# A planned residual quantizer: one PSUM pool, larger score tiles, strict turns on the DMA queues

## The chip, the cores and the metric

The kernel runs on one core of a Trainium2 chip. The metric is the device time of one execution in microseconds. The core has five engines that run side by side: TensorE (PE in the profile, its weight loads PEld), VectorE (DVE), ScalarE (ACT), GpSimd (POOL) and SyncE (SP). Each carries out its own instructions in the order in which they were written, and waits for the others by semaphores. Sixteen DMA engines, which all queues share, move data between the device memory and the on-chip memory (SBUF). Matmul results go to PSUM, a small memory of eight banks of 2 KB a partition, from which DVE or ACT must take them away.

## The reference

Two signals of 16,000 tokens with 512 features pass through a three-tap convolution over time, feature by feature, and SiLU. Four stages of vector quantization follow: each finds the nearest of eight code words to what is left, and subtracts it. The sum of the chosen words goes through a second three-tap convolution.

```
xp = jnp.pad(x, ((0,0),(pad,pad),(0,0)))
for i in range(K):                       # K = 3
    z = z + xp[:, i:i+T, :] * dw_enc[i][None, None, :]
z = jax.nn.silu(z)
res = z; q = 0
for s in range(Nq):                      # Nq = 4 stages, C = 8 words each
    cb = codebooks[s]
    d2 = |res|^2 - 2 res.cb + |cb|^2     # [B, T, C]
    sel = cb[d2.argmin(-1)]
    q = q + sel; res = res - sel
qp = jnp.pad(q, ((0,0),(pad,pad),(0,0)))
for i in range(K):
    y = y + qp[:, i:i+T, :] * dw_dec[i][None, None, :]
```

(x is 2 x 16,000 x 512; everything is bf16.)

## The kernel before, in words

The 32,000 tokens are laid out as 128 partitions of 250 consecutive tokens. A *group* g is the g-th token of every partition, so 128 tokens; a *chunk* is up to 16 groups (`SIZES`: 12, then fourteen times 16, then 14). The 512 features are four tiles of 128.

*Loading.* `XT` holds a chunk and one more group on either side with features on the partitions. It comes by transposing DMAs on SP's queue (L486), four groups to a DMA, so five a chunk with the last one half as large; `xpool` has two `XT`. The first chunk comes another way: `XR` is loaded as it lies (L291, one DMA on SP's queue, and the two edge pieces on ACT's, L294), PE transposes it (L454) into PSUM, and ACT (L461) and DVE (L459) copy it to `XT`, two of the four feature tiles each.

*Front, a chunk and feature tile at a time.* Three products with the taps on DVE (L553), two sums, either on DVE (L561) or as an accumulating DMA from POOL's queue (L559; all four first sums and one of the second sums in every chunk but the first, so 75 in all), Exp, Ln and Exp on ACT (L565, L573, L576) with an addition of one on DVE between (L569), and the product on DVE (L581), which gives the residual `RES`.

*A stage.* `score` (L629) multiplies, on PE, each half group of residuals with itself and with the code words beside it; a large negative mask (L637) leaves only the diagonal in play, so that a maximum (L651, DVE) is the squared length. L654 copies the dot products. Short DVE instructions (L673 to L697) make the one-hot of the nearest word; PE transposes it (L707), DVE copies it to `OHT` (L714). Then the word is subtracted for each pair of quarter chunks and feature tile: either PE adds both in PSUM (L752, L731, tile `NEW`) and ACT copies the result back (L758), or PE makes only the word (`SEL`) and DVE adds (L747). `ON_DVE` says how many go each way.

*Output.* `finish` multiplies the one-hots with tables of decoder tap times code word (L785, tile `Y`), ACT copies to `YSB` (L791), SP stores four groups at once (L795).

*PSUM.* `psG` has two tiles of one bank for scores, with up to `GB` = 6 groups each, so a 16-group stage uses three (6, 5, 5). `psA` has three tiles of two banks for all else.

*The order* is written out by a planner. Each piece of work is a task with an engine, a guessed cost, what it needs, which buffers it takes and gives back, and a due time. `Plan.run` schedules all tasks forward and backward several times with random shifts (`ROUNDS`: seed, spreads, passes), and `emit` writes the instructions in the order of the planned starts. On the queues shared by transposes and accumulating DMAs the planner asks for a distance `APART` between the two kinds. `keep_apart` (L409) makes it a real dependency: a DMA of one kind waits for the one `LAG` places back among those of the other kind already written. Where the plan leaves PE idle, `emit` fills in matmuls whose results nobody reads (L430), if a score bank is planned free and PE was planned busy for less than `WARM` of the last 4 us; `ahead` does the same once at the start (L439).

Of the kernel before, what the change touches and what calls it, by code (L numbers as in the profile page):

```python
# [21 lines left out]
GB = 6  # L22
# [10 lines left out]
WARM = 0.6  # L33
# [8 lines left out]

ZB, TB, EB, LNB, YB = 4, 5, 3, 1, 3
# [3 lines left out]
ROUNDS = [(940, 0.3, 0.0, 7), (4101, 0.3, 2.0, 9), (5991, 0.3, 0.0, 7), (15520, 0.3, 0.0, 10)]  # L47
# [6 lines left out]
APART, CLUMP = 0.5, 2.0  # L54

LAG = 2


class Plan:
# [18 lines left out]
    def pass_over(self, rank, backward=False):  # L78
# [99 lines left out]
    def emit(self, starts, order):  # L178
        tasks = self.tasks
        free, back, spans, end = self.slots["psG"], [], [], 0.0  # L180
        for n in order:
            engine, hold, delay, _, _, emit, take, give, _, _ = tasks[n]
            at = starts[n]
            if engine == "PE":
                while end + 0.3 <= at:
# [3 lines left out]
                    while spans and spans[0][1] < end - 4.0:  # L189
                        spans.pop(0)  # L190
                    if free > 0 and sum(b - max(a, end - 4.0) for a, b in spans) < 4.0 * WARM and self.idle():
                        spans.append((end, end + 0.3))
                        end += 0.3
                    else:
                        end += 0.1
# [5 lines left out]
            free -= take.count("psG")  # L201
            for _ in range(give.count("psG")):
                heapq.heappush(back, at + max(hold, delay))
# [4 lines left out]
def kernel(  # L208
# [32 lines left out]
    psG = ctx.enter_context(tc.tile_pool(name="psG", bufs=2, space=bass.MemoryType.PSUM))  # L241
    psA = ctx.enter_context(tc.tile_pool(name="psA", bufs=3, space=bass.MemoryType.PSUM))
# [25 lines left out]
    def tap_columns():  # L268
        pst = psA.tile([P, 2, 512], F32, name="ps_w", tag="psa")
# [6 lines left out]
    plan = Plan({"XT": 2, "Z": ZB, "T": TB, "E": EB, "LN": LNB, "Y": YB, "psG": 2, "psA": 3, "RES": 3, "KEY": 3,  # L276
# [22 lines left out]
    def code_words():  # L299
        pst = psA.tile([P, 2, 512], F32, name="ps_cbt", tag="psa")  # L300
# [13 lines left out]
    def code_norms():  # L314
# [12 lines left out]
        psg = psA.tile([P, 2, 512], F32, name="ps_g", tag="psa")  # L327
# [69 lines left out]
    ident, book = landed(1.8), landed(9.3)  # L397
    taps_in = setup(0.2, 0.4, [ident, landed(3.0)], early, tap_columns)
# [24 lines left out]
    pending = []  # L423

    def warm():
        if not scored[2:]:
            return False
        if not pending:
            pending.append(psG.tile([P, 512], F32, name="PS"))
        nc.tensor.matmul(pending[0][:, 0:GB * HT].rearrange("p (r c) -> p r c", c=HT), lhsT=IDENT, rhs=MASK, start=True, stop=True,  # L430
                         skip_group_check=True)
# [4 lines left out]
    def ahead():  # L436
        pending.append(psG.tile([P, 512], F32, name="PS"))
        for _ in range(AHEAD):
            nc.tensor.matmul(pending[0][:, 0:P], lhsT=IDENT, rhs=IDENT, start=True, stop=True, skip_group_check=True)  # L439

    plan.add("PE", 0.1 * AHEAD, 0.1 * AHEAD, [taps_in], early, ahead)

    def load_rows(st, org):
# [6 lines left out]
        def turn(i):  # L450
            pst = psA.tile([P, 2, 512], F32, name="ps_x", tag="psa")
            st["ps", i] = pst.rearrange("p b n -> p (b n)").bitcast(BF16)
            for n in range(G + 2):
# [9 lines left out]
        rows = st["rows"] = plan.add("LOAD", 0.0, 1.2 + 0.46 * (G + 2), [], early, room, take=("XT",))  # L463
        for i in range(KT):
            t = plan.add("PE", 0.11 * (G + 2), 0.11 * (G + 2) + 0.2, [rows, ident], early, lambda i=i: turn(i),
                         take=("psA",))
# [423 lines left out]
```

## Time and profile before

| | us |
|---|---|
| median of the three timed runs | 745.02 (744.42 to 745.52) |
| profiled execution | 742.04 |
| its span | 740.3 |
| DVE busy | 685.9 |
| ACT busy | 665.4 |
| PE busy, weight loads | 590.8, 314.2 |
| POOL busy | 81.7 |
| mean granted PE clock | 0.934 |

The span runs from the first to the last instruction of the execution. Busy is the time in which an engine carries out at least one instruction; of PE it says little, since its matmuls are pipelined. In a group's row the columns are the line, engine and operation, output and input with their shapes, the count, then busy time and mean duration of one in ns, then the idle time of the engine just before them and what ended it. A wait's row gives who waited for whom, the total in us, how often, and the longest.

### The profile page before, as it was taken

Reading aid. Unit: us, or ns where it says so; the run is one execution under the profiler, and the core shown is the slowest. Engines: PE = TensorE matmul, PEld = TensorE weight load, DVE = VectorE, ACT = ScalarE, POOL = GpSimd, SP = SyncE. Lnnn points to the kernel's source line nnn. Section 1 sums busy time; section 2 is a strip of 40 time slices with the busy share of each in tenths; the row PEclk is TensorE's granted clock in tenths of the full one; section 3 lists DMA queues with packets and bytes.
Section 4 is the critical chain, followed back from the end, with each engine's and each line's share of the span. In section 5 each row is a group of like instructions: output and inputs, shape, how many; then the busy total and the mean of one; then the engine's idle time right before and its main releaser. Section 6 shows DMA issues by size and latency. Waiting matters only on the chain. (4 is left out here: it accounts for less than half of the span.)

```text
span 740.3 us, 23586 instructions
## 1 busy us (share of the span) xinstructions
PE 590.8 (80%) x10478; PEld 314.2 (42%) x10544; DVE 685.9 (93%) x1359; ACT 665.4 (90%) x539; POOL 81.7 (11%) x104
## 2 busy tenths in 40 slices
PE   5037687787987888986978888878988898989996
PEld 5023334344444444434444444444453444444543
DVE  6999989899999999997999999989999999998952
ACT  2688979899999999998899999989999999976576
POOL 3112101111101011100101111100111101100000
PEclk9566969999999999999799899999999999999999
DMA  7969795859696967839978875959896435320234
GB/s 178 189 130 182 135 200 104 141 122 201 182 174 158 209 133 164 165 116 143 188 171 177 175 165 143 182 132 174 172 210 136 131 64 152 87 88 2 88 143 199
DMA packets 160833, 111.14 MB, mean 150 GB/s; under 512 B 142426, under 2 KB 142811, under 8 KB 160603
## 3 DMA queue, kind: packets, MB, share of 16 engines
q1 hardware_dynamic: 148976, 69.61, 39.5%
q0 software_dynamic: 11472, 39.76, 29.9%
q8 instruction: 82, 1.34, 0.8%
q10 hardware_dynamic: 282, 0.26, 0.1%
q14 instruction: 21, 0.16, 0.1%
HBM read 2.39 MB, written 32.77 MB: 47 GB/s over the span
## 5 line engine op out<-in xcount | busy, mean ns | idle before, releaser
L758 ACT ACTIVATE RES<-NEW 128x1024 bf16<-128x1024 f32 (+1 forms) x218 | 218.5, 1043 | 28.6 <-PE NEW L731 21.9
L747 DVE TENSOR_TENSOR RES<-RES,SEL 128x1024 bf16<-128x1024 bf16 (+1 forms) x166 | 197.5, 1203 | 6.7 <-PE SEL L731 6.3
L643 PE MATMUL PS<-RES 128*64 128x80 bf16 (+1 forms) x8064 | 176.1, 203 | 11.2 <-DVE RES L581 9.7
L643 PEld LDWEIGHTS <-RES 128*64 128x64 bf16 x8064 | 172.8, 115 | 19.6 <-DVE RES L581 10.6
L752 PE MATMUL NEW<-RES,IDENT 128*128 128x512 bf16 (+1 forms) x436 | 137.7, 399 | 31.3 <-ACT RES L758 15.6
L791 ACT ACTIVATE YSB<-Y 128x1024 bf16<-128x1024 f32 (+1 forms) x126 | 126.6, 1061 | 8.4 <-PE Y L785 4.5
L565 ACT ACTIVATE E<-Z 128x2048 bf16<-128x2048 bf16 (+1 forms) x64 | 123.2, 1931 | 11.5 <-DMA Z<-T 4.0
L559 POOL DMA_DIRECT2D Z<-T x75 | 72.9, 976 | 537.5 <-ACT RES L758 78.8
L573 ACT ACTIVATE LN<-E 128x2048 f32<-128x2048 bf16 (+1 forms) x64 | 123.0, 1923 | 9.9 <-DVE E L569 9.2
L576 ACT ACTIVATE E<-LN 128x2048 bf16<-128x2048 f32 (+1 forms) x64 | 123.0, 1922 | 0.4
L651 DVE TENSOR_REDUCE TR<-PS 128x5 bf16<-128x320 f32 (+1 forms) x188 | 96.0, 515 | 14.4 <-PE PS L643 14.3
L553 DVE TENSOR_SCALAR T<-XT,WENC 128x2048 bf16<-128x2048 bf16 (+1 forms) x128 | 94.8, 745 | 5.1 <-DMA Z<-T 5.1
L731 PEld LDWEIGHTS <-CBN 32*128 32x128 bf16 x768 | 32.6, 92 | 137.7 <-issue 134.3
L785 PE MATMUL Y<-A,OHT 128*128 128x512 bf16 x219 | 77.6, 382 | 16.4 <-ACT RES L758 6.0
L731 PE MATMUL NEW<-OHT,CBN 32*128 32x512 bf16 (+1 forms) x436 | 88.3, 402 | 0.1
L581 DVE TENSOR_TENSOR RES<-Z,E 128x2048 bf16<-128x2048 bf16 (+1 forms) x64 | 77.3, 1208 | 0.0
L731 PE MATMUL SEL<-OHT,CBN 32*128 32x512 bf16 (+1 forms) x332 | 58.7, 396 | 22.0 <-ACT RES L758 13.3
L637 PE MATMUL PS<-MASK,IDENT 128*64 128x320 bf16 (+1 forms) x376 | 64.6, 340 | 8.6 <-DVE PR L654 6.2
L561 DVE TENSOR_TENSOR Z<-Z,T 128x2048 bf16<-128x2048 bf16 (+1 forms) x53 | 62.5, 1181 | 2.7 <-DMA Z<-T 2.7
L752 PEld LDWEIGHTS <-IDENT 128*128 128x128 bf16 x436 | 33.1, 99 | 67.4 <-issue 57.4
L430 PE MATMUL PS<-MASK,IDENT 128*128 128x384 bf16 x167 | 46.2, 359 | 10.1 <-DVE PR L654 9.8
L785 PEld LDWEIGHTS <-OHT 128*128 128x128 bf16 x373 | 32.1, 97 | 50.8 <-issue 22.8
(78 smaller groups left out, 416.2 us busy)
## 6 DMA issues: line engine op xcount, KB each, us to landing
Z<-T POOLq DMA_DIRECT2D x75, 512.0 KB, 5.6
out_dram<-YSB SPq DMA_DIRECT2D x61, 512.0 KB, 3.2
RES<-in_x_dram SPq DMA_DIRECT2D x1, 1664.0 KB, 6.8
XT<-in_x_dram SPq DMA_TRANSPOSE x74, 5.7
out_dram<-YSB SPq DMA_DIRECT2D x1, 384.0 KB, 2.3
out_dram<-YSB SPq DMA_DIRECT2D x1, 256.0 KB, 2.7
A<-in_dw_dec_dram POOLq DMA_DIRECT2D x2, 96.0 KB, 6.4
CB<-in_codebooks_dram ACTq DMA_DIRECT2D x1, 128.0 KB
```

The source lines that it names most:

```text
L553: nc.vector.tensor_scalar(out=places(u[name]), in0=taps(i, k), scalar1=WENC[:, i, k:k + 1], scalar2=None, op0=ALU.mult)
L565: nc.scalar.activation(u["E"][:, 0:G, :], u["Z"][:, 0:G, :], ACT.Exp, scale=-1.0)
L573: nc.scalar.activation(u["LN"][:, 0:G, :], u["E"][:, 0:G, :], ACT.Ln)
L576: nc.scalar.activation(u["E"][:, 0:G, :], u["LN"][:, 0:G, :], ACT.Exp, scale=-1.0)
L643: nc.tensor.matmul(V[h * HT:(h + 1) * HT, r, :], lhsT=half[:, LC:LC + HT], rhs=half[:, lo:hi], start=False, stop=(i == KT - 1), skip_group ...
L651: nc.vector.tensor_reduce(out=u["TR"][:, q:q + m], in_=u["V", q][:, :, own:own + HT], axis=AX.X, op=ALU.max)
L731: nc.tensor.matmul(ps, lhsT=CBN[s][rows, i * P:(i + 1) * P], rhs=u["OHT"][rows, 0:MB, :], start=start, stop=True, skip_group_check=True)
L747: nc.vector.tensor_tensor(out=old, in0=old, in1=u["SEL", i, j][:, :, 0:W].rearrange("p h (m t) -> p h m t", t=HT), op=ALU.add)
L752: nc.tensor.matmul(NEW[:, h, 0:W], lhsT=IDENT, rhs=tokens(i, j + h, 1), start=True, stop=False, skip_group_check=True)
L758: nc.scalar.activation(old, u["NEW", i, j][:, :, 0:W].rearrange("p h (m t) -> p h m t", t=HT), ACT.Copy)
L785: nc.tensor.matmul(Y[:, h, :], lhsT=lhs(), rhs=rhs, start=(a == 0), stop=(a == len(terms) - 1))
L791: nc.scalar.activation(u["YSB"][:, k:k + n, :], u[k][:, 0:n, :], ACT.Copy)
```

## The change

- PSUM is one pool `psA` of four tiles of two banks. `bank(name)` gives every user its tile; it returns the tile that a filler matmul has opened, if there is one.
- `GB` is 4 groups to a bank, and a score tile has two banks: 16 groups take two tiles of 8, 12 take two of 6. The reduction and the copy each run over both banks at once.
- `LAG` is 1: a transpose waits for the last accumulating DMA written before it, and the other way round. The planner's `APART` has a value for each kind, and its costs for a run of transposes are lower.
- The rows of the first chunk come in two halves on SP's queue, after the two edge pieces, which have moved there from ACT's queue. PE transposes the first half of each feature tile when that has come. One of the four copies to `XT` is DVE's, three are ACT's.
- Filler matmuls are 512 columns wide, take a tile of the common pool, and are put in if PE was planned busy for less than 0.75 of the last 3.4 us. `ahead` no longer waits for the taps.
- Seeds, and guessed costs of loads, are new, so the order of work is new on every engine.

```diff
-GB = 6
+GB = 4
-WARM = 0.6
+WARM, WINDOW, TICK = 0.75, 3.4, 0.22
+FIRST_ROWS, ALL_ROWS = 7.8, 10.0
-ROUNDS = [(940, 0.3, 0.0, 7), (4101, 0.3, 2.0, 9), (5991, 0.3, 0.0, 7), (15520, 0.3, 0.0, 10)]
+ROUNDS = [(667, 5.0, 0.0, 4), (2210, 0.3, 2.0, 7), (7052, 1.0, 0.0, 2)]
-APART, CLUMP = 0.5, 2.0
-LAG = 2
+APART = (0.0, 1.9, 2.3)
+CLUMP = 2.0
+LAG = 1
...
-                                lost = max(0.0, APART - (now - ended))
+                                lost = max(0.0, APART[sort if backward else kind] - (now - ended))
...
-    psG = ctx.enter_context(tc.tile_pool(name="psG", bufs=2, space=bass.MemoryType.PSUM))
-    psA = ctx.enter_context(tc.tile_pool(name="psA", bufs=3, space=bass.MemoryType.PSUM))
+    psA = ctx.enter_context(tc.tile_pool(name="psA", bufs=4, space=bass.MemoryType.PSUM))
+    pending = []
+    def bank(name):
+        return pending.pop() if pending else psA.tile([P, 2, 512], F32, name=name, tag="psa")
...
-    nc.sync.dma_start(out=XR[:, 1:G + 2, :], in_=xv[:, 0:G + 1, :])
     for b in range(B):
         p = b * HB
-        nc.scalar.dma_start(out=XR[p + 1:p + HB, 0, :], in_=xv[p:p + HB - 1, S - 1, :])
+        nc.sync.dma_start(out=XR[p + 1:p + HB, 0, :], in_=xv[p:p + HB - 1, S - 1, :])
+    HALF = (G + 2) // 2
+    for a, b in ((1, HALF), (HALF, G + 2)):
+        nc.sync.dma_start(out=XR[:, a:b, :], in_=xv[:, a - 1:b - 1, :])
...
-        nc.tensor.matmul(pending[0][:, 0:GB * HT].rearrange("p (r c) -> p r c", c=HT), lhsT=IDENT, rhs=MASK, start=True, stop=True,
-                         skip_group_check=True)
+        nc.tensor.matmul(pending[0][:, 0, :], lhsT=IDENT, rhs=CB4, start=True, stop=True, skip_group_check=True)
...
-            if i % 2:
+            if i == 0:
                 nc.vector.tensor_copy(st["XT"][:, 0:G + 2, i, :], src)
...
-                done.append(plan.add("DMA", 0.7 * m, 2.7 + 0.7 * m, [room], due, lambda n=n, m=m: run(n, m), mode=RUNS))
+                done.append(plan.add("DMA", 0.6 * m, 2.4 + 0.6 * m, [room], due, lambda n=n, m=m: run(n, m), mode=RUNS))
...
-            PS = pending.pop() if pending else psG.tile([P, 512], F32, name="PS")
-            V = u["V", q] = PS[:, 0:m * (hi - lo)].rearrange("p (r c) -> p r c", r=m)
-            for h in range(2):
-                nc.tensor.matmul(V[h * HT:(h + 1) * HT, :, own:own + HT], lhsT=IDENT[:, h * HT:(h + 1) * HT], rhs=MASK[:, 0:m, :],
-                                 start=True, stop=False, skip_group_check=True)
+            PS = bank("PS")
+            V = u["V", q] = PS[:, :, 0:m // 2 * (hi - lo)].rearrange("p b (r c) -> p b r c", c=hi - lo)
+            for b in range(2):
+                for h in range(2):
+                    nc.tensor.matmul(V[h * HT:(h + 1) * HT, b, :, own:own + HT], lhsT=IDENT[:, h * HT:(h + 1) * HT],
+                                     rhs=MASK[:, 0:m // 2, :], start=True, stop=False, skip_group_check=True)
...
-            nc.vector.tensor_reduce(out=u["TR"][:, q:q + m], in_=u["V", q][:, :, own:own + HT], axis=AX.X, op=ALU.max)
+            nc.vector.tensor_reduce(out=u["TR"][:, q:q + m].rearrange("p (b r) -> p b r", b=2), in_=u["V", q][:, :, :, own:own + HT], axis=AX.X, op=ALU.max)
...
-            nc.vector.tensor_copy(u["PR"][:, q:q + m, :], u["V", q][:, :, pick:pick + C])
-        banks = -(-G // GB)
+            nc.vector.tensor_copy(u["PR"][:, q:q + m, :].rearrange("p (b r) c -> p b r c", b=2), u["V", q][:, :, :, pick:pick + C])
+        banks = -(-G // (2 * GB))
```

All other users of PSUM (`ps_w`, `ps_cbt`, `ps_g`, `ps_x`, `ps_oh`, `SEL`, `NEW`, `Y`) call `bank` in place of `psA.tile`.

More of the change, by code (lines that the diff above doesn't have):

```diff
@@ L188, in emit @@
                         heapq.heappop(back)
-                    while spans and spans[0][1] < end - 4.0:
+                    while spans and spans[0][1] < end - WINDOW:
                         spans.pop(0)
[L191 to L195, printed above, removed]
+                    if (free > 0 and "psA" in take and sum(b - max(a, end - WINDOW) for a, b in spans) < WINDOW * WARM
+                            and self.idle()):
+                        spans.append((end, end + TICK))
+                    end += TICK
                 while back and back[0] <= at:
@@ L200, in emit @@
                 spans.append((at, end))
-            free -= take.count("psG")
-            for _ in range(give.count("psG")):
+            free -= take.count("psA")
+            for _ in range(give.count("psA")):
                 heapq.heappush(back, at + max(hold, delay))
```

64 lines of the change are left out of this document (33 added, 31 removed).

## The prediction

> **What bounds the kernel now.** I read the page's busy table first, then the same by stages, then what the two full engines wait for, then the DMA landings, then the granted clock. The page, with its two rows of slices for clock and DMA:
>
> ```profile
> span 740.3 us, 23586 instructions
> PE 590.8 (80%) x10478; PEld 314.2 (42%) x10544; DVE 685.9 (93%) x1359; ACT 665.4 (90%) x539; POOL 81.7 (11%) x104
> ...
> PEclk9566969999999999999799899999999999999999
> DMA  7969795859696967839978875959896435320234
> ```
>
> VectorE (DVE) is nearly full and ScalarE (ACT) almost as full. The table by stretches says where the rest is:
>
> ```profile
> 0.00:60.00 60.00, 20.94 (x235) 16.48 (x235) 52.37 (x109) 36.07 (x23) 14.85 (x31) 0.71 0.83 166
> 60.00:340.00 280.00, 231.41 (x4197) 119.80 (x4216) 273.10 (x530) 269.49 (x214) 31.99 (x35) 0.94 0.79 157
> 340.00:360.00 20.00, 14.73 (x171) 6.15 (x169) 14.62 (x29) 15.43 (x13) 2.58 (x3) 0.74 1.08 185
> 360.00:623.00 263.00, 222.51 (x4107) 119.28 (x4139) 256.94 (x503) 255.62 (x208) 29.18 (x33) 0.97 0.73 156
> 623.00:740.30 117.30, 101.21 (x1785) 52.50 (x1792) 88.84 (x192) 88.76 (x85) 3.11 (x3) 0.99 0.30 105
> ```
>
> Columns: stretch and length, busy time of PE, weight loads, DVE, ACT, POOL, then clock, DMA share, GB/s. From 60 to 623 us DVE idles 18.3 us and ACT 22.5 us of 563: two engines bound it jointly, and relief of one is worth only what the other follows. The start costs ACT 23.9 us; the tail costs each 28.5 us, a chain through PE. The waits, of DVE, ACT and SP's queue:
>
> ```profile
> DVE T L553 <- DMA Z<-T: 5.1, 4, 4.2
> DVE Z L561 <- DMA Z<-T: 2.7, 2, 2.5
> ```
> ```profile
> ACT RES L758 <- PE NEW L731: 21.9, 24, 2.4
> ACT E L565 <- DMA Z<-T: 4.0, 2, 2.5
> ```
> ```profile
> SPq L486 <- DMA Z<-T: 100.7, 18, 13.7
> ```
>
> Late accumulating DMAs ("adds") cost 11.8 us on the two full engines; SP's 100.7 us before transposes is hidden by the double buffer XT. The landings (SP's transposes, then POOL's adds):
>
> ```profile
> L486 SPq DMA_TRANSPOSE XT<-in_x_dram x74: 1232/3008/8887, 9.4 to 554.9; - x74
> DMA to landing us min/median/max: 3.4/5.7/10.2
> ```
> ```profile
> DMA to landing us min/median/max: 4.5/5.6/12.3
> ```
>
> An add alone lands in 4.5 us, a four-group transpose in 4.5 (3.4 is a two-group one); medians 1.1 to 1.2 above and maxima of 10 to 12 are what they cost each other. The 12.3 us add was issued at 333.5, 0.3 us behind a transpose; with it DVE stood 4.2 us at 345.8, the largest hole of the middle.
>
> **The change part by part.** Working against the profiled execution: 742.04 us, span 740.3 and 1.7 around it. The three timed runs have a median of 745.02, so 3.0 are added at the end.
>
> *Score tiles of 8 groups.* A 16-group stage has two reductions (L651) and two copies (L654) in place of three each (6, 5, 5); the 12-group chunk's 6 and 6 stay.
>
> ```profile
> L651 DVE TENSOR_REDUCE TR<-PS 128x5 bf16<-128x320 f32 x120 | 58.6, 492 | 8.2 <-PE PS L643 8.1
> L651 DVE TENSOR_REDUCE TR<-PS 128x6 bf16<-128x384 f32 x68 | 37.8, 556 | 6.3 <-PE PS L643 6.2
> ...
> L654 DVE CAST PR<-PS 128x40 bf16<-128x40 f32 x120 | 23.7, 198 | 0.0
> ...
> L654 DVE CAST PR<-PS 128x48 bf16<-128x48 f32 x68 | 14.0, 206 | 0.0
> ```
>
> A group more costs a reduction 64 ns and a copy 8, so eight cost 684 and 222 ns. DVE's next instruction starts some 0.09 us before the last one ends (152.74 + 0.49 against 153.14 in the timeline), so by occupied time a stage falls from 0.47 + 2 x 0.40 + 0.12 + 2 x 0.11 = 1.61 us to 2 x (0.59 + 0.135) = 1.45. 60 stages x 0.16 = 10 us less on DVE. ACT gets no relief, so the worth lies between 0 and -10; because ACT has 22.5 us of idle to give up there, I take -6. The coarser last tile is exposed where a stage runs alone: 64 matmuls in place of 40 (0.65 us) is +0.4, reduction and copy +0.2, less the reduction that no longer queues (-0.4): +0.2 us in some five tail stages, +1 (0 to +3). PE: mask columns stay 2,048 a stage, in 8 matmuls for 6; PE is no bound there. Nothing.
>
> *One pool of four double tiles.* Before: three for residuals, one-hots and outputs, two single banks for scores; now a score tile waits in the same queue as the rest. PE's waits for buffers (matmuls behind ACT's or DVE's eviction) sum to about 80 us, mostly harmless; 21.9 us of ACT's own waits for NEW could shrink, or grow when a score tile holds a slot for some 3 us. Occupancy by rows: 8 score tiles x 3 us, 14 NEW x 2.5, 10 SEL x 2.2, 8 Y x 2.5 and 4 one-hots x 1 make 105 of 4 x 42 us a chunk, 62%; before 81 of 3 x 44, 61%. Zero, bounds -6 to +6.
>
> *Strict turns.* Each transpose waits for the last add issued, each add for the last transpose (before: for the one before the last). In the changed order the kind changes 67 times, before 53. Prices: three transposes with nothing beside them took SP 6.49 us (295.17), 2.2 each, half runs 1.25; adds in a row land 2.75 apart (302.39 and 304.07 land at 307.31 and 310.06); a turn adds landing less pace, 1.8 to 2.3. Sum: 59 x 2.2 + 15 x 1.25 + 75 x 2.75 + 67 x 2.0 = 489 us, against some 600 us of DVE work until the last Exp: 31 us a chunk, up to 40 in some, of 40 to 44. It fits, with little left. Queued behind the waits: on SP the stores (4 a chunk) and later transposes, on POOL the next adds; DVE waits for adds (T buffers, Z) and ACT for Z. Best: the 11.8 us of late adds go. Worst: stores, 2.6 us each alone, lie wholly between the turns: 31 + 10 = 41 a chunk, in the six fullest 50, of which the Z and T buffers cover half: +15. I take -4: a third of the late adds goes, since they came from overlap that can't happen now.
>
> By the Trainium skill (DMA: Bandwidth & Descriptors, Rules for kernel authors) a transpose beside ordinary DMAs needs no wait; by that rule this part would buy nothing and cost its turns, and the sum would be some 4 us higher or more. The rows agree on throughput: a transpose and an add issued together at 461.6 and 462.1 both land at 469.8, 8.2 us, against 9.0 in turn. They disagree on spread, as the 12.3 us shows.
>
> *First rows in halves.* Before, PE's transposes waited until 9.26 us for edge rows queued last, and DVE stood 5.63 us until 11.17 behind ps_cbt. Now edges go first and PE starts on half. DVE's order puts code norms (1.75 us), the second code columns (1.2) and one copy of XT (1.0) ahead of the products and loses the other copy (1.0) to ACT, where 1.66 us more fall into its idle start. With code words landed at 8.5 us as before, products begin near 15.1 instead of 13.7, but 4.9 us of work are done: -3.5 (bounds -5 to +1).
>
> *Warm-up matmuls.* The order has 79 of 512 columns for 167 of 384, and 73 of the 79 belong to the first three chunks; the middle had about eight a chunk and gets six in all. The clock:
>
> ```profile
> 295.00:298.40 3.40, 1.88 (x21) 0.83 (x16) 3.40 (x6) 3.40 (x4) 0.00 (x0) 1.00 1.29 163
> 298.40:301.80 3.40, 3.40 (x49) 1.80 (x48) 3.40 (x7) 3.40 (x4) 0.00 (x0) 0.50 1.02 226
> ```
>
> After 3.4 us with PE 55% busy the clock is halved for the next 3.4; this happened six times between 131 and 623 us, after such stretches at 12 to 57%, each with about 1 us of waits on DVE or ACT. Eight fewer fillers of 0.28 us a chunk may bring six more: 0 to +10 us, taken as +3, because PE waiting for buffers is ahead of its users. The skill (TensorE: Matmul & The Clock Gate, HAM oscillation) bids to avoid PE gaps over about 3.4 us; by it only the 12% stretch would count and this term be 0. The trace differs: 55% was enough.
>
> *Planner.* Costs and seeds are new, so every order is. The tail has the same 66 ACT instructions after the last Exp and 131 DVE ones for 149. Zero, +/-5.
>
> Sum: -6 + 1 + 0 - 4 - 3.5 + 3 + 0 = -9.5; 742.0 - 9.5 = 732.5, with 3.0 for the median 735.5.
>
> **The rivals.** *The turns bind (slower).* Place: the POOL queue, adds behind transposes that SP holds behind a store waiting for ACT. For it: 31 of 42 us a chunk without stores, and SP already stands 329.6 us for YSB. Against: only 7.9 us of POOL's waits were for a transpose. It decides from a term of +5.5; at +15 for -4 the sum is +9.5: 754.5. Chance 0.18. *Clock.* With 20 more halvings in the middle, 1 us each, +20 for +3: +7.5, 752.5; it decides from about 13 more. The 0.6 to 0.75 stretches that now stay at full clock speak for it. 0.11. *All of it counts.* ACT follows DVE's 10 us, late adds all go (-11.8), the clock holds: -10 + 1 - 11.8 - 3.5 = -24: 721. Against: ACT 96% busy in the middle. 0.14. *It cancels.* The terms end within 1.5 us of zero (0.2%, about what this measurement can tell from no change): 745. 0.05. My forecast has 0.52, by itself 726 to 743.
>
> **How the numbers follow.** Faster: 0.52 + 0.14 = 0.66, less 0.02 for the forecast's edge and a bad order: 0.64; same 0.05; slower 0.18 + 0.11 + 0.02 = 0.31. The range reaches to the rivals on both sides: 721 to 757.
>
> **What would show it.** Right: 128 reductions near 0.66 us; adds' and transposes' medians near 4.5 and maxima under 8; POOL's waits for transposes grown from 7.9 us but DVE's and ACT's for adds not above 11.8; DVE busy near 675; first Exp no later than 20 us and fourth L581 near 41 instead of 44.7; middle clock 0.9 or more. Wrong: DVE or ACT waiting over 20 us for adds, or a clock under 0.9 in the middle with ACT waiting for NEW.

## The result and the profile after

The changed kernel takes 768.5 us (four runs, 765.55 to 772.1), against 745.27 (744.42 to 747.95) for the kernel before in the same measurement: 1.0308 times as long, with a 95% interval of 1.0255 to 1.036. The forecast was 735.5, with a range up to 757: wrong in sign, and the time lies outside the range. The profiled execution took 769.49 us with a span of 767.2, 26.9 us more than the 740.3 before. Times here and below are medians of all runs of a kernel, while ratios leave out runs that lie over 1.5% above its fastest.

The page of the changed kernel, busy times and the slices of the clock:

```profile
span 767.2 us, 23622 instructions
...
PE 611.4 (80%) x10592; PEld 323.6 (42%) x10592; DVE 683.0 (89%) x1234; ACT 670.2 (87%) x540; POOL 78.4 (10%) x105
...
PEclk9578759889879898969989989899978789889998
```

DVE is busy for 2.9 us less and ACT for 4.8 more, so nearly the whole loss is idle time: on DVE 84.2 us where it was 54.4, on ACT 97.0 where it was 74.9. The row of clock digits no longer stands at 9 in the middle. The same stretches as before (columns: stretch and length, busy time of PE, weight loads, DVE, ACT and POOL, then clock, DMA share, GB/s):

```profile
0.00:60.00 60.00, 24.40 (x257) 17.91 (x258) 50.00 (x102) 37.02 (x25) 13.10 (x31) 0.77 0.89 155
60.00:340.00 280.00, 232.16 (x3811) 114.61 (x3812) 257.98 (x456) 256.39 (x203) 29.35 (x33) 0.83 0.74 152
340.00:360.00 20.00, 16.25 (x386) 11.32 (x380) 18.00 (x35) 18.68 (x14) 1.70 (x2) 0.86 0.67 171
360.00:623.00 263.00, 214.70 (x3848) 113.77 (x3848) 244.41 (x433) 245.06 (x199) 29.96 (x34) 0.89 0.72 156
623.00:767.20 144.20, 123.90 (x2308) 65.97 (x2304) 112.57 (x212) 113.09 (x103) 4.25 (x5) 0.91 0.31 102
```

From 60 to 623 us DVE now idles 42.6 us instead of 18.3 and ACT 42.9 instead of 22.5. The last 144 us are not slower, only longer, because more of the work is left by then. The Exps (L574 after, L565 before) are a good ruler for that, as there are 64 of them, spread over all chunks. In the list of that line's instructions (mean, with shortest and longest, then start of the first and the last):

```profile
L574 ACT ACTIVATE E<-Z x64: 1467/1910/2020, 24.5 to 672.8; 128x2048 bf16<-128x2048 bf16 x60, 128x1536 bf16<-128x1536 bf16 x4
```
```profile
L565 ACT ACTIVATE E<-Z x64: 1467/1932/2147, 18.4 to 645.6; 128x2048 bf16<-128x2048 bf16 x60, 128x1536 bf16<-128x1536 bf16 x4
```

The first fence is the kernel after, the second the one before. The first Exp is 6.1 us late, the 16th 10.6 (143.3 for 132.7), the last 27.2, and from there to the end it is 94.4 us against 94.6. So some 11 us are lost by 143 us, some 17 between there and the last Exp, nothing in the tail.

What DVE, ACT, SP's queue and POOL waited for after the change (who, for whom, total us, times, longest):

```profile
DVE TR L661 <- PE PS L653: 36.7, 46, 2.2
DVE Z L570 <- DMA Z<-T: 10.2, 8, 2.8
...
DVE T L562 <- DMA Z<-T: 2.3, 1, 2.3
```
```profile
ACT RES L768 <- PE NEW L741: 22.2, 29, 2.7
ACT YSB L801 <- PE Y L795: 21.6, 23, 3.0
...
ACT E L574 <- DMA Z<-T: 3.1, 2, 2.7
```
```profile
SPq L494 <- DMA Z<-T: 347.4, 32, 19.6
```
```profile
POOL Z L568 <- DMA XT<-in_x_dram: 61.6, 5, 16.6
```

The large new items are DVE's first row and ACT's second. In the kernel before they read:

```profile
DVE TR L651 <- PE PS L643: 14.3, 14, 3.4
```
```profile
ACT YSB L791 <- PE Y L785: 4.5, 9, 1.0
```

The reduction waited 14 times for score matmuls, now 46 times; the copies of outputs waited 9 times, now 23 times. ACT's wait for `NEW` has hardly changed (21.9 us before). All of DVE's waits for PE went from 31.8 to 48.4 us, ACT's from 45.6 to 70.7. From 60 us to the last Exp alone, DVE waits 31.5 us for PE where it was 10.1, and ACT 36.3 where it was 12.0. The waits of SP and POOL for each other's DMAs, which the strict turns make, grew by far more (SP from 100.7 to 347.4, POOL from 7.9 to 61.6), but what reaches the two full engines is 15.6 us of late adds against 11.8.

What PE waited for in the kernel after; the rows that tell the story are those where a matmul waits for a buffer:

```profile
PE NEW L762 <- ACT RES L768: 19.2, 25, 3.2
...
PE PS L647 <- ACT RES L768: 5.4, 5, 1.8
...
PE NEW L762 <- DVE PR L664: 4.4, 6, 1.5
```

In the kernel before the mask matmuls that open a score tile (PS, there L637) waited only for DVE's copy of an older score tile, and `NEW` or `Y` never for that copy:

```profile
PE PS L637 <- DVE PR L654: 6.2, 12, 1.1
```

Now a score tile waits for ACT, and a `NEW` for DVE's score copy. PE's waits as a whole hardly grew: from 60 us to the last Exp they are 97.6 us where they were 89.9, of which 48.9 and 51.0 for ACT. What is new is who waits for whom. One such place, from the timeline at 384 us (start, duration, engine, line, operation; in brackets the wait in front of it):

```profile
384.39 1.91 ACT L574 ACTIVATE E<-Z 128x2048 bf16<-128x2048 bf16 x1
...
386.19 1.02 ACT L768 ACTIVATE RES<-NEW 128x1024 bf16<-128x1024 f32 x1
...
387.27 1.01 PE L762 MATMUL NEW<-RES,IDENT 128*128 128x512 bf16 x2 [3.20 <-ACT RES L768]
...
388.75 0.64 PE L647 MATMUL PS<-MASK,IDENT 128*64 128x256 bf16 x4
...
389.18 2.34 PE L653 MATMUL PS<-RES 128*64 128x80 bf16 x64
...
391.57 0.69 DVE L661 TENSOR_REDUCE TR<-PS 128x8 bf16<-128x512 f32 x1 [2.02 <-PE PS L653]
...
393.82 1.31 PE L653 MATMUL PS<-RES 128*64 128x80 bf16 x64
```

ACT has an Exp ahead of the copy that gives a tile back. PE stands 3.20 us for that tile, and the score matmuls for DVE are queued behind. From 386.4 us the clock is halved for two windows, so 64 score matmuls take 2.34 us (the same number at full clock, at 393.82 us, takes 1.31), and DVE stands 2.02 us. How the clock goes down is seen in windows of 3.4 us (columns as above):

```profile
209.00:212.40 3.40, 2.01 (x12) 0.49 (x11) 3.40 (x9) 3.40 (x5) 0.35 (x1) 1.00 0.81 154
212.40:215.80 3.40, 3.21 (x20) 1.09 (x20) 3.40 (x7) 2.92 (x3) 0.00 (x0) 0.50 0.36 79
215.80:219.20 3.40, 3.40 (x70) 2.49 (x64) 2.44 (x4) 2.26 (x2) 0.85 (x1) 0.50 1.10 383
```

A window with PE 59% busy is followed by two at half clock. Between 131 and 690 us there are 20 halvings with 143.4 us at half clock, where the kernel before had 6 with 30.7; the mean granted clock is 0.865 for 0.934.

The start did not go as forecast either. PE and DVE in the timeline of the first 20 us:

```profile
11.60 0.18 PE L336 MATMUL ps_g<-DIAG,ONES 32*128 32x32 bf16 x1 [5.37 <-DVE DIAG L334]
11.71 1.67 PE L461 MATMUL ps_x<-IDENT,RES 128*128 128x128 bf16 x14
```
```profile
10.24 0.68 DVE L327 CUSTOM_DVE_ANT_0 JUNK<-CB 32x512 bf16<-32x512 bf16 x1 [3.68 <-DMA CB<-in_codebooks_dram]
...
18.45 1.14 DVE L562 TENSOR_SCALAR T<-XT,WENC 128x1536 bf16<-128x1536 bf16 x2
```

The code words land at 10.2 us (8.5 before), and DVE's code norms wait 3.68 us for them. In PE's queue one small matmul of those norms (`ps_g`) stands ahead of the transposes of the first rows, so these begin at 11.71 us (before: 9.26), although both halves of the rows are there by then, landed 5.0 and 8.0 us after their issue at 1.5 and 1.9. Products begin at 18.45 us (before 13.71).

### The profile page after: what moved, and what is told of

Its sections match the earlier page's. It is cut to its first block, busy times and chain, and to the rows that moved or that the text cites. A ratio compares the mean times of both kernels' runs of the same rounds, so it can differ in the third digit from the quotient of the medians.

```text
span 767.2 us, 23622 instructions
## 1 busy us (share of the span) xinstructions
PE 611.4 (80%) x10592; PEld 323.6 (42%) x10592; DVE 683.0 (89%) x1234; ACT 670.2 (87%) x540; POOL 78.4 (10%) x105
## 4 chain that ended last, share of the span: by engine, by line
PE 32%; DVE 28%; ACT 18%; DMA 15%; issue 4%; SPq 2%; ACTq 0%; POOLq 0%; DVEq 0%; POOL 0%
PE PS L653 11%; DMA Z<-T 9%; PE NEW L762 8%; DVE RES L757 7%; ACT RES L768 6%; DMA XT<-in_x_dram 5%; ACT YSB L801 5%; PE NEW L741 4%; PE Y L795 4%; DVE T L562 4%; DVE RES L590 3%; DVE TR L661 3%; DVE Z L570 3%; PE PS L647 3%; ACT E L574 3%
## 5 line engine op out<-in xcount | busy, mean ns | idle before, releaser
L768 ACT ACTIVATE RES<-NEW 128x1024 bf16<-128x1024 f32 (+1 forms) x216 | 213.5, 1025 | 31.1 <-PE NEW L741 22.2
L653 PEld LDWEIGHTS <-RES 128*64 128x64 bf16 x8064 | 177.6, 121 | 36.7 <-DVE RES L590 26.5
L762 PE MATMUL NEW<-RES,IDENT 128*128 128x512 bf16 (+1 forms) x432 | 154.3, 445 | 40.3 <-ACT RES L768 19.2
L574 ACT ACTIVATE E<-Z 128x2048 bf16<-128x2048 bf16 (+1 forms) x64 | 121.0, 1894 | 10.4 <-DVE Z L570 6.2
L568 POOL DMA_DIRECT2D Z<-T x75 | 68.9, 958 | 580.9 <-ACT YSB L801 87.8
L661 DVE TENSOR_REDUCE TR<-PS 128x8 bf16<-128x512 f32 (+1 forms) x128 | 86.7, 678 | 37.2 <-PE PS L653 36.7
L795 PE MATMUL Y<-A,OHT 128*128 128x512 bf16 x247 | 86.1, 398 | 15.7 <-ACT YSB L801 4.4
L741 PE MATMUL NEW<-OHT,CBN 32*128 32x512 bf16 (+1 forms) x432 | 96.4, 442 | 0.1
L741 PE MATMUL SEL<-OHT,CBN 32*128 32x512 bf16 (+1 forms) x330 | 62.9, 424 | 28.6 <-ACT RES L768 10.7
L762 PEld LDWEIGHTS <-IDENT 128*128 128x128 bf16 x436 | 33.2, 101 | 94.6 <-issue 82.4
L570 DVE TENSOR_TENSOR Z<-Z,T 128x2048 bf16<-128x2048 bf16 (+1 forms) x53 | 62.3, 1178 | 10.2 <-DMA Z<-T 10.2
L647 PE MATMUL PS<-MASK,IDENT 128*64 128x256 bf16 (+1 forms) x512 | 56.6, 303 | 13.8 <-ACT RES L768 5.4
L795 PE MATMUL Y<-B,OHT 128*128 128x512 bf16 x122 | 48.2, 395 | 0.1
```

The lines of the kernel that those rows point to most:

```text
L574: nc.scalar.activation(u["E"][:, 0:G, :], u["Z"][:, 0:G, :], ACT.Exp, scale=-1.0)
L653: nc.tensor.matmul(V[h * HT:(h + 1) * HT, r // (m // 2), r % (m // 2), :], lhsT=half[:, LC:LC + HT], rhs=half[:, lo:hi], start=False, stop ...
L661: nc.vector.tensor_reduce(out=u["TR"][:, q:q + m].rearrange("p (b r) -> p b r", b=2), in_=u["V", q][:, :, :, own:own + HT], axis=AX.X, op= ...
L741: nc.tensor.matmul(ps, lhsT=CBN[s][rows, i * P:(i + 1) * P], rhs=u["OHT"][rows, 0:MB, :], start=start, stop=True, skip_group_check=True)
L762: nc.tensor.matmul(NEW[:, h, 0:W], lhsT=IDENT, rhs=tokens(i, j + h, 1), start=True, stop=False, skip_group_check=True)
L768: nc.scalar.activation(old, u["NEW", i, j][:, :, 0:W].rearrange("p h (m t) -> p h m t", t=HT), ACT.Copy)
```

## The experiments

"Planned anew" says that a kernel's buffers or seeds differ, so that the planner wrote another order; elsewhere the order is the same, instruction by instruction, apart from fillers. Every ratio is to the kernel before, timed beside it, with its 95% interval. Halvings are counted from 131 to 690 us. Not every seed leads the planner to an order with given buffers, so some kernels have seeds of their own.

### The clock

`before_nofill` takes every filler out of the kernel before, whose order is kept:

```diff
-WARM = 0.6
+WARM = 0.0
```

> The kernel before, same order of work, with its 167 filler matmuls left out. Theory clock: the fillers are what holds the middle at full clock; without them the mean clock falls from 0.934 to about 0.86 as in the changed kernel, halvings between 131 and 690 us go from 6 to 15 or more, DVE's and ACT's waits for PE grow by 15 us together or more, and the time is 755 to 768 us. Theory turns and theory pool: the fillers are off the path, the time stays within 4 us of 745.

`before_fill75` puts the changed kernel's rule for fillers into the kernel before (268 fillers for 167), and `before_fill90` the same with a share of 0.9 (329):

```diff
-WARM = 0.6
+WARM, WINDOW, TICK = 0.75, 3.4, 0.22
...
-                    if free > 0 and sum(b - max(a, end - 4.0) for a, b in spans) < 4.0 * WARM and self.idle():
-                        spans.append((end, end + 0.3))
+                    if free > 0 and sum(b - max(a, end - WINDOW) for a, b in spans) < WINDOW * WARM and self.idle():
+                        spans.append((end, end + TICK))
```

> The kernel before, same order, with more fillers: put in below 0.75 of 3.4 us as the changed kernel asks, into the score banks, 268 in place of 167. Theory clock: the clock rises from 0.934 to 0.95 or more, the six halvings of the middle become three or fewer, and the time falls by 2 to 6 us. Theory pool or turns: no change within 2 us, or some us slower because fillers stand in the way of real matmuls.

> The kernel before, same order, fillers up to a planned share of 0.9 of 3.4 us: 329 for 167. With 268 the clock was 0.954 and the time 0.63% below before. If the clock is what they buy, it rises to 0.96 or more and the time is 733 to 739 us; if the last ones only stand in the way, 740 or more.

`after_fillany` lets the changed kernel fill whenever PE is planned idle, also where no tile is planned free (361 fillers for 79):

```diff
-                    if (free > 0 and "psA" in take and sum(b - max(a, end - WINDOW) for a, b in spans) < WINDOW * WARM
+                    if ("psA" in take and sum(b - max(a, end - WINDOW) for a, b in spans) < WINDOW * WARM
```

> The changed kernel, same order, with fillers put in wherever the plan has PE idle and below 0.75, whether or not it has a tile free: 361 for 79. On the chip they wait for the tile like the matmuls behind them. Theory clock: the mean clock rises from 0.865 to 0.93 or more and the time falls by 8 us or more. Theory pool (waits for tiles, not the clock, make PE late): fillers behind a taken tile only delay what follows, the time stays at 768 or grows by up to 10 us.

| | fillers | median us | ratio | clock | halvings (us) | DVE waits for PE |
|---|---|---|---|---|---|---|
| before_nofill | 0 | 751.7 | 1.0094 (1.0059 to 1.013) | 0.881 | 19 (88.7) | 46.8 |
| before | 167 | 742.9 to 745.6 | 1 | 0.934 | 6 (30.7) | 31.8 |
| before_fill75 | 268 | 737.83 | 0.9937 (0.9896 to 0.9979) | 0.954 | 5 (17.1) | 31.2 |
| before_fill90 | 329 | 736.28 | 0.9888 (0.9813 to 0.9963) | 0.952 | 5 (17.1) | 33.8 |
| after | 79 | 768.5 | 1.0308 (1.0255 to 1.036) | 0.865 | 20 (143.4) | 48.4 |
| after_fillany | 361 | 761.36 | 1.0252 (1.0195 to 1.031) | 0.963 | 5 (20.5) | 43.7 |

Without fillers the kernel before has nearly as many halvings as the changed one, but 88.7 us at half clock where that has 143.4, and loses 0.9%, not 3%. That lies between what the theories had asked for. With the clock brought up from 0.865 to 0.963 the changed kernel is still 2.5% slower than before, and its interval overlaps that of the plain one: a gain of 4 us by the ratios, 7 by the medians. This is no upper bound for the clock, since the new fillers themselves wait 53 us for tiles, ahead of real matmuls. Another estimate comes from `before_nofill`: 0.9% for 58 us more at half clock makes 1.8%, or 14 us, for the 113 us more of the changed kernel. DVE's main wait in `after_fillany`, at a higher clock than in the profile of the kernel before, is

```profile
DVE TR L661 <- PE PS L653: 25.0, 31, 2.6
```

so much of PE's lateness stays at a high clock: from 60 us to the last Exp DVE waits 26.0 us for PE and ACT 31.6, where the changed kernel has 31.5 and 36.3 and the kernel before 10.1 and 12.0. The clock rival had the right mechanism (few fillers, many halvings). It is a part of the loss, which these two ways put at 4 to 14 of the 23 us.

### The strict turns

`before_lag1` puts the strict turns alone into the kernel before, `after_lag2` takes them alone out of the changed one:

```diff
-LAG = 2
+LAG = 1
```
```diff
-LAG = 1
+LAG = 2
```

> The kernel before, same order, with strict turns alone. Theory turns: 755 us or more, DVE's and ACT's waits for adds grow from 11.8 us to over 20. Theory clock or pool: 742 to 750, clock 0.92 to 0.94; landings' maxima fall below 9 us.

> The changed kernel, same order, only that a transpose or an add waits for the one before the last of the other kind, as before. Theory turns: 755 us or less, and POOL's 61.6 us of waits for transposes go. Theory clock and theory pool: within 4 us of 768.5, clock still 0.85 to 0.87; the waits of DVE and ACT for adds (15.6 us in all in the changed kernel) change by less than 5 us.

In the kernel before they cost 4.8%: 779.08 us, ratio 1.0484 (1.0412 to 1.0556). In the changed kernel taking them out gives no gain but a loss of about one point: 774.78, ratio 1.0424 (1.0379 to 1.0469). What DVE and ACT of `before_lag1` waited for:

```profile
DVE Z L561 <- DMA Z<-T: 26.1, 12, 3.9
DVE T L553 <- DMA Z<-T: 12.9, 4, 5.4
```
```profile
ACT E L565 <- DVE Z L561: 22.2, 9, 5.3
ACT E L565 <- DMA Z<-T: 16.2, 4, 7.6
```

Single waits are long, up to 3.9 to 7.6 us: DVE waits 40.9 us for DMAs (7.8 in the kernel before), and Exp stands behind. So the turns can bind, at over twice the price that the forecast gave as their worst. In `after_lag2` DVE's waits for DMAs do fall, from 16.6 to 6.4 us, but its waits for PE rise from 48.4 to 64.7, and ACT's for PE from 70.7 to 77.7. What held the changed kernel was elsewhere. With both the turns loosened and the clock brought up (`after_lag2_fillany`, the two edits shown) it is the same:

> The changed kernel, same order, with fillers wherever the plan has PE idle (clock 0.96) and the looser turns. If turns were hidden only because a slow PE left the DMA queues time, loosening them must now help: 750 or less against 761.4 with strict turns. If the common pool alone sets the pace, 758 to 768.

767.2 us, ratio 1.0269 (1.0207 to 1.0331), at a clock of 0.953: no better than `after_fillany`.

### The common pool

`before_pool8` is the kernel before with the PSUM part alone: one pool of four double tiles and score tiles of 8 groups. Turns, first rows and the threshold for fillers stay, but a filler now takes a tile of the common pool, and the plan has room for 87 of them instead of 167; it is planned anew. The core of the edit:

```diff
-GB = 6
+GB = 4
...
-    psG = ctx.enter_context(tc.tile_pool(name="psG", bufs=2, space=bass.MemoryType.PSUM))
-    psA = ctx.enter_context(tc.tile_pool(name="psA", bufs=3, space=bass.MemoryType.PSUM))
+    psA = ctx.enter_context(tc.tile_pool(name="psA", bufs=4, space=bass.MemoryType.PSUM))
+    pending = []
+    def bank(name):
+        return pending.pop() if pending else psA.tile([P, 2, 512], F32, name=name, tag="psa")
...
-    plan = Plan({"XT": 2, "Z": ZB, "T": TB, "E": EB, "LN": LNB, "Y": YB, "psG": 2, "psA": 3, "RES": 3, "KEY": 3,
+    plan = Plan({"XT": 2, "Z": ZB, "T": TB, "E": EB, "LN": LNB, "Y": YB, "psA": 4, "RES": 3, "KEY": 3,
```

> The kernel before with one part of the change alone: one pool of four double tiles, score tiles of eight groups, fillers taken from that pool (87 of them, for 167). The order is planned anew with the seeds of before; the planner's own end is the same as before's (729.8 against 729.6 us). Theory pool and clock (the common pool leaves no free tile for fillers, so the clock falls and PE is late): 757 to 772 us, clock 0.85 to 0.88, DVE's waits of L651's successor for PE at 30 us or more. If the pool part is worth what its DVE work says, 735 to 742 us, and the loss sits in the turns, the start or the new order.

778.52 us, ratio 1.0517 (1.044 to 1.0593). The pool alone, without the strict turns, costs as much as the whole change or more. What DVE waited for, and PE's waits across the two kinds of users:

```profile
DVE TR L654 <- PE PS L646: 35.1, 37, 2.7
```
```profile
PE SEL L734 <- ACT YSB L794: 9.5, 12, 2.0
...
PE SEL L734 <- DVE PR L657: 3.8, 6, 0.9
...
PE NEW L755 <- DVE PR L657: 2.9, 3, 1.4
PE PS L640 <- ACT RES L761: 2.7, 4, 1.3
```

These are the same pairs as in the changed kernel: the reduction waits for scores, a score tile for ACT, `SEL` and `NEW` for DVE's score copy. Two things are mixed in it, the larger score tile and the sharing, and two kernels part them. `before_pool6` has the common pool with the old score tiles of 6, 5 and 5 groups (each in one bank of a double tile), and `before_g1d` has the 8-group tiles and four double tiles, but one is for scores alone and three for the rest:

```diff
-ROUNDS = [(940, 0.3, 0.0, 7), (4101, 0.3, 2.0, 9), (5991, 0.3, 0.0, 7), (15520, 0.3, 0.0, 10)]
+ROUNDS = [(20, 0.3, 2.0, 5)]
...
-            PS = pending.pop() if pending else psG.tile([P, 512], F32, name="PS")
+            PS = bank("PS")[:, 0, :]
```
```diff
-ROUNDS = [(940, 0.3, 0.0, 7), (4101, 0.3, 2.0, 9), (5991, 0.3, 0.0, 7), (15520, 0.3, 0.0, 10)]
+ROUNDS = [(21, 0.3, 0.0, 5)]
...
+    def bank(name):
+        if name == "PS":
+            return pending.pop() if pending else psG.tile([P, 2, 512], F32, name=name, tag="psg")
+        return psA.tile([P, 2, 512], F32, name=name, tag="psa")
```

> The kernel before with the common pool of four double tiles, but score tiles of 6, 5 and 5 groups in one bank of such a tile; planner's own end 736.2 us, one round of seed 20. Theory shared pool (a score tile holds a slot that NEW, SEL or Y then wait for): DVE's waits for PE at 45 us or more as in all kernels with this pool, time 765 to 785. Theory coarse tile (DVE waits because 64 matmuls come before its first reduction): DVE's waits for PE fall back to 30 to 37 us and the time is no more than 8 us above the reseeded kernel before.

> The kernel before with the same four double tiles and the same score tiles of eight groups as the run of the common pool alone, but three of them for all else and one for scores only. Planner's own end 732.6 us (seed 21); the common pool's was 729.8 and the chip made 772.0 of it. Theory sharing (a tile waits for a slot that the other engine must free, so DVE and ACT hold each other up through PE): span 745 to 758, DVE's waits for PE under 40 us. Theory number of tiles (four in flight are too few, five were there before): 765 or more, DVE's waits for PE at 48 or more.

`before_pool6` takes 781.19 us, ratio 1.0489 (1.0398 to 1.0579): with the old score tiles the common pool costs the same, so the coarse tile is not the cause. It is also the cleaner case: in `before_pool8` DVE waits 21.0 us for DMAs as well (7.8 in the kernel before), for which its new order may be the reason; in `before_pool6` it waits 2.6 us for DMAs, and 63.6 for PE. Both have few fillers and a lower clock (0.876 and 0.880); by the estimate above, the 112.6 us at half clock of `before_pool6` are worth 1.3 of its 4.9 points. `before_g1d` takes 759.16, ratio 1.019 (1.0164 to 1.0216): three points of the five are gone with one tile set apart, with a clock of 0.921. DVE and PE of `before_g1d`:

```profile
DVE TR L657 <- PE PS L649: 26.8, 28, 3.2
```
```profile
PE PS L643 <- DVE PR L660: 15.5, 20, 1.5
```

A single dedicated tile still makes scores wait for their own copies, but no score tile is opened behind ACT any more.

`after_split` undoes the PSUM part in the changed kernel (two single banks for scores, three double tiles for the rest, `GB` = 6; planned anew, strict turns kept), and `after_split_lag2` loosens the turns as well, in the same order:

```diff
-GB = 4
+GB = 6
-ROUNDS = [(667, 5.0, 0.0, 4), (2210, 0.3, 2.0, 7), (7052, 1.0, 0.0, 2)]
+ROUNDS = [(43, 0.3, 0.0, 5), (101, 0.3, 0.0, 6)]
...
-    psA = ctx.enter_context(tc.tile_pool(name="psA", bufs=4, space=bass.MemoryType.PSUM))
+    psG = ctx.enter_context(tc.tile_pool(name="psG", bufs=2, space=bass.MemoryType.PSUM))
+    psA = ctx.enter_context(tc.tile_pool(name="psA", bufs=3, space=bass.MemoryType.PSUM))
```

> The changed kernel with its PSUM part undone: three double tiles and two single banks, score tiles of 6, 5 and 5, fillers (315) in the score banks; strict turns, the halved first rows and the new costs stay. Seeds that give a plan were needed; the planner rates it 733.9 us. Theory pool and clock: clock 0.93 or more, time 740 to 752 us. Theory turns or start: 760 us or more with the clock at 0.93.

> The changed kernel with its PSUM part undone, same order as that run, and the looser turns of before. In that run DVE waited 35.9 us for adds and transposes, ACT 5.1. Theory turns (a strict wait costs where the order has no room for it): DVE's waits for DMA fall below 15 us and the time from 770 to 755 or less. Otherwise within 4 us of 770, and the new order itself is slow.

`after_split` takes 770.06 us, ratio 1.0353 (1.0288 to 1.0419), `after_split_lag2` 741.35, ratio 0.996 (0.9927 to 0.9994). What DVE waited for, first of `after_split`, then of `after_split_lag2`:

```profile
DVE T L564 <- DMA Z<-T: 24.8, 9, 7.1
DVE TR L662 <- PE PS L654: 13.9, 14, 3.3
DVE Z L572 <- DMA Z<-T: 11.1, 9, 4.2
```
```profile
DVE TR L662 <- PE PS L654: 13.5, 12, 3.3
DVE T L564 <- DMA Z<-T: 9.3, 3, 3.9
```

With the pools separate the score waits are back at the 14 us of the kernel before, and then the strict turns cost four points again, as late adds. All else of the change (first rows in halves, the new fillers and guessed costs, and the order that comes of them) is harmless when taken together. The four cases side by side, as ratios to the kernel before:

| | loose turns | strict turns |
|---|---|---|
| separate pools | 0.996 (after_split_lag2) | 1.0353 (after_split) |
| one pool | 1.0424 (after_lag2) | 1.0308 (after) |

Either part alone costs some 30 us, and both together no more than one. The clock does not make the difference between the pools: `after_lag2_fillany`, with one pool and loose turns, has a clock of 0.953 and a ratio of 1.0269, three points above `after_split_lag2` with 0.946. That the turns cost nothing more beside the pool fits DVE's waits: with one pool and strict turns 48.4 us for PE and 16.6 for DMAs (in `after_reseed` 59.0 and 5.9), with separate pools and strict turns 29.7 and 35.9. Where PE is already late, the adds have time to land. This is a reading of the waits; one pool was run without the strict turns in one order of the changed kernel only.

### How much an order is worth

Several of these kernels are planned anew, so the price of a new order by itself has to be known. `before_reseed` and `before_reseed2` change only the seeds of the kernel before, `after_reseed` those of the changed one:

```diff
-ROUNDS = [(940, 0.3, 0.0, 7), (4101, 0.3, 2.0, 9), (5991, 0.3, 0.0, 7), (15520, 0.3, 0.0, 10)]
+ROUNDS = [(38, 0.3, 2.0, 5)]
```
```diff
-ROUNDS = [(940, 0.3, 0.0, 7), (4101, 0.3, 2.0, 9), (5991, 0.3, 0.0, 7), (15520, 0.3, 0.0, 10)]
+ROUNDS = [(25, 0.3, 0.0, 5)]
```
```diff
-ROUNDS = [(667, 5.0, 0.0, 4), (2210, 0.3, 2.0, 7), (7052, 1.0, 0.0, 2)]
+ROUNDS = [(56, 0.3, 2.0, 5)]
```

> The kernel before with another order: one planner round of seed 38, which the planner rates 732.7 us against 729.6 for the order of before. It says how much a new order of the same structure may cost. If orders of one structure differ little, 742 to 752 us; if the seeds of before were picked for the chip and any other order loses, 760 us or more, and then the new order alone explains most of the change's loss.

> The kernel before with a third order: one planner round of seed 25, which the planner rates 733.2 us. Together with seed 38 (span 752.5 for a planned 732.7) it says how far orders of equal rating lie apart on the chip: 745 to 760 if a new order by itself costs up to some 15 us, 765 or more if the common pool's loss is no larger than that of any other order.

> The changed kernel with another order: planner seeds exchanged for a single round of seed 56, which the planner itself rates 732.2 us against 725.0 for the changed kernel's order. If the loss lies in the change's structure, 765 to 785 us and a clock again below 0.88; if the order on record was an unlucky one, 757 us or less.

| | turns | end by the planner, us | span, us | ratio |
|---|---|---|---|---|
| before | loose | 729.6 | 740.3 | 1 |
| before_reseed | loose | 732.7 | 752.5 | 1.0162 (1.0049 to 1.0275) |
| before_reseed2 | loose | 733.2 | 749.8 | 1.0104 (1.0037 to 1.017) |
| after_split_lag2 | loose | 733.9 | 741.8 | 0.996 (0.9927 to 0.9994) |
| before_g1d, one tile for scores | loose | 732.6 | 757.1 | 1.019 (1.0164 to 1.0216) |
| after_split, separate pools | strict | 733.9 | 770.3 | 1.0353 (1.0288 to 1.0419) |
| before_pool8, one pool | loose | 729.8 | 772.0 | 1.0517 (1.044 to 1.0593) |
| before_pool6, one pool | loose | 736.2 | 772.7 | 1.0489 (1.0398 to 1.0579) |
| after, one pool | strict | 725.0 | 767.2 | 1.0308 (1.0255 to 1.036) |
| after_reseed, one pool | strict | 732.2 | 768.5 | 1.044 (1.0365 to 1.0515) |

A new order of the unchanged structure costs 1.0 and 1.6%; together with the original and `after_split_lag2` the four lie 2 points apart. `before_g1d` at 1.9% is hardly outside of that, so the price of one dedicated double tile in place of two single ones is not told from that of an order. The four orders with one pool (1.031 to 1.052) all lie beyond. The planner does not see it: it expected 725.0 us of the changed kernel, its best figure of all, and the chip added 42. It adds 8 to 20 with separate pools and loose turns, 24 with one score tile set apart, and 36 to 42 with one pool or strict turns.

`split_lag2_fill90` is `after_split_lag2` with the stronger fillers (389), as an attempt at a faster version:

```diff
-WARM, WINDOW, TICK = 0.75, 3.4, 0.22
+WARM, WINDOW, TICK = 0.9, 3.4, 0.22
```

> The changed kernel with PSUM part and strict turns undone, same order as those runs, and fillers up to a planned share of 0.9: 389 for 315. By what more fillers brought the kernel before (268: -0.63%, 329: -1.1%), 735 to 740 us against 741.4; 741 or more if its clock of 0.946 has nothing left to give.

747.5 us, ratio 1.0035 (0.9997 to 1.0073), in spite of a clock of 0.963, which only `after_fillany` has too. The fillers that help the kernel before do not help this order. The fastest version stays `before_fill90`, ratio 0.9888 (0.9813 to 0.9963), 736.28 us: the kernel before with nothing but more fillers.

## Why the prediction was wrong, step by step

- *Score tiles of 8 groups* (-6, from 10 us less on DVE). The price of one was right: reductions take 687 ns where 684 was forecast, copies 217 where 222. But DVE's busy time fell by 2.9 us, not by 10. The reductions' and copies' rows alone fell by some 20 us (133.5 to 113.6). The trace shows where the rest went: the durations of all DVE instructions sum to 25.9 us less (774.6 for 800.5), but the time in which neighbours overlap fell by 23.1 us (91.6 for 114.7). There are 125 instructions fewer, whose overlap the forecast had counted, but also 60 more holes (150 for 90), across which nothing overlaps. The coarse tile itself does no harm (`before_pool6` is as slow as `before_pool8`), and the tail is unchanged (94.4 us for 94.6).

- *One pool of four double tiles* (0, bounds -6 to +6). This is the step that failed. In the changed kernel's setting it takes 33 us (`after_lag2` against `after_split_lag2`, 1.0424 and 0.996), in the kernel before some 35, its toll on the clock included; of either number an order may account for up to 15. The working compared the share of time for which tiles are held, 62 and 61%, and took equal shares for equal waits. The share says nothing of who waits for whom. Before, a score tile came free through DVE, on which it depends anyway; in the common pool it comes free through whoever has the oldest tile, as at 384 us through ACT behind a 1.9 us Exp, and PE's queue stops there with everything behind it. (That the sharing causes the loss is shown by `before_pool8`, `before_pool6` and `after_split_lag2`. How it comes about is read from that place and from the new pairs in PE's waits, and is not shown as a whole: PE's waits in sum hardly grew, so how single stops add up to some 30 us stays open.) The prediction read the row "ACT waits for NEW" and asked if it would shrink; it did not ask which new pairs of engines the common pool couples. A dedicated tile gives back about three points, part of them by the clock; how the tiles are handed out in detail, by planned and by real order, was not tried.

- *Strict turns* (-4, bounds -11.8 to +15). Wrong by itself: +36 us in the kernel before, +29 with the PSUM part undone. The sum of 31 to 40 us a chunk said that throughput fits, and it does; the engines wait for single adds, up to 4 to 8 us each. So the rival on turns had the right kind of loss but less than half the price. In the changed kernel the cost does not show, which fits a PE that is late itself: the late adds that reach DVE and ACT are 15.6 us, 3.8 more than before, and the landings improved only in part:

```profile
L494 SPq DMA_TRANSPOSE XT<-in_x_dram x74: 1232/2212/9124, 2.4 to 606.8; - x74
DMA to landing us min/median/max: 3.3/4.8/11.1
```
```profile
DMA to landing us min/median/max: 4.5/5.2/10.1
```

The transposes' median fell from 5.7 to 4.8 and the adds' from 5.6 to 5.2 (4.5 was forecast for both), and the maxima are 11.1 and 10.1, not under 8. The kernels with separate pools show what the wait buys: 4 to 5% more time. The rule of the Trainium skill (DMA: Bandwidth & Descriptors, Rules for kernel authors), that a transpose next to ordinary DMAs needs nothing, stood against this step in the prediction. The rule is about correct results and gives no time, so it could not price the step. In these runs the transposes need no wait for speed either: with separate pools it made the kernels 4.8 and 3.9 points slower. The prediction set one add of 12.3 us against that, which was too little.

- *First rows in halves* (-3.5, bounds -5 to +1). Wrong: products began at 18.45 us, not 15.1, and the first Exp at 24.5, not by 20. The step assumed code words at 8.5 us as before; they landed at 10.2, though issued at 1.4 us in both kernels, and why was not tested. It also followed DVE's order and PE's order each by itself, and missed that PE's transposes stand behind `ps_g`, which waits for DVE, which waits for the code words. What it cost at the end was not measured apart: `after_split_lag2` has these loads too, with its first Exp at 21.3 us (18.4 in the kernel before), and is 0.4% faster than that.

- *Warm-up matmuls* (+3, bounds 0 to +10). Right in kind: 14 more halvings, worth 4 to 7 us by `after_fillany` and some 14 by the estimate from `before_nofill`. The middle's clock came out at 0.83 and 0.89, under the 0.9 that the prediction named as a sign of failure.

- *Planner* (0, bounds -5 to +5). The bounds were too narrow. Orders of one structure lie up to 2 points, some 15 us, apart, though the planner rates them within 4.3 us.

- *What bounds the kernel.* The reading held, with a lesson in it: DVE and ACT bound the middle jointly, 18.3 and 22.5 us of idle in 563. An edit can relieve such a pair by little, but a late PE costs both: their idle time there grew to 42.6 and 42.9 us.

## What to carry to other kernels

When one pool of PSUM takes the place of two, list for every user who gives its tile back, and look for pairs that did not wait for each other before; the share of time that tiles are held does not show them. A wait that keeps two kinds of DMA apart is priced by how late a single transfer comes and who stands for it, not by whether all transfers fit. And before a part of a change is judged through a planner, measure what a new seed alone does.

## What the runs showed of the hardware

PE's clock is halved on far less than an idle window: windows of 3.4 us with PE 55 and 59% busy were followed by half clock. Filling such gaps with matmuls that nobody reads is worth 0.9% (from 0 fillers to 167) and up to 1.1% more (329) in the kernel before; in the order of `after_split_lag2`, 74 more fillers gained nothing. And two losses of about 30 us, a late PE and late adds, did not add up here: together they cost 23 us.
